# Sending the softmax reciprocals with each token's id, and a new order on VectorE behind attention, in a fused attention and mixture-of-experts kernel

## The chip, the cores and the metric

The kernel runs on one core of one Trainium2 chip. The metric is the time of one execution on the device in microseconds (us). Engines are called by the profile's letters: PE is TensorE (PEld its weight loads), DVE is VectorE, ACT is ScalarE, POOL is GpSimd, SP is the SyncE queue, which only issues DMAs here.

## What is computed

```python
def _attn_ref(q, k, v, cap):                 # 8 batches, 12 heads, 448 positions, 64 wide
    scores = scale * np.matmul(q, k.transpose(0, 1, 3, 2))
    scores = cap * np.tanh(scores / cap)
    ...
    attn = attn / (np.sum(attn, axis=-1, keepdims=True) + 1e-09)
    return np.matmul(attn, v)
def _moe_ref(x, w_gate, w1, w2):             # 3584 tokens of 768, 8 experts, F = 1024
    expert_idx = np.argmax(x @ w_gate, axis=1)
    ...
    for e in range(E):
        h = np.maximum(x[mask] @ w1[e], 0.0)
        out[mask] = gate_w[mask, None] * (h @ w2[e])
```

The output of attention, with its 12 heads side by side, is the input `x` of the experts.

## The kernel before, in words

**Attention.** The 8 batches are cut into 24 quads of four heads, a quad into 7 tiles of 64 keys. A step is two tiles. In each step PE makes two tiles of scores (`scores`, L249), ACT a tanh on each (`tanh`, L262) and one exponential on both (`expo`, L265), and PE the product with V of earlier tiles (`pv`, L315). Two score tiles fit in PSUM, so PE can be ahead of ACT by that much and no more. DVE adds the exponentials up for the softmax sums (`adds`, L270). The output is left unnormalised: the sums of a batch are made by `strips0` and `strips`, turned by `rec_t`, and `rec_v` takes their reciprocals (`rec`, one for each head and position) and scales the logits `lt` by them. What comes then is entered in `tasks` under a step and run there.

**Reciprocals before.** `rec_p` spreads the reciprocals by three products of 128x56 into PSUM, and `rec_c` copies them behind the 192 columns of `yt`, the turned output of the batch. `store` writes `yt` to the scratch table `xd` in DRAM, rows of 198 floats. So whoever gathers rows of `xd` (`load_x`) gets the six reciprocals of a row with it, and `scale_c`, `scale_k` multiply them in.

**Routing.** `log_p` makes the logits, `route_v` the expert of each token (`ob`), `route_s` and `route_g` its gate, `place_p` and `place_v` its slot, and four `place_d` scatter the token's id and gate (`tokg`) into the table `ids`, 8 bytes a row, by POOL's queue. A block of up to 448 tokens of one expert starts with `load_ids` (a gather of `ids` into `idt`), then `make_idx` on DVE (`xi`, from `idt`), then `load_x`.

**Experts.** Each block takes eight `up` (f = 0 to 7: 18 products for one slice of 128 hidden units, into `ph`) and eight `down` (18 products, into y). All operands are split in a high and a low part, so a product is (high, high), (high, low), (low, high): the third of each group needs the low part of a weight. ACT makes high parts (`high`, L797) and relu (L936), DVE low parts (`low`, L802, tiles w10l to w17l and w20l to w27l) and the hidden low parts (L937). Large blocks stream 448 columns, the two small ones at the end 256 (`up`) and 384 (`down`, L964). In `down` of a small block the hidden tile in `hb` is the stationary operand and the weight the moving one; elsewhere the weight is stationary.

**Behind attention.** The first block (j = -2, tokens of the first three batches) is run while the last batch is still being routed: its eight `up` stand between steps of the routing, in an order that is written out by hand (L1126 to L1186 before). Each engine works its own instructions in that order, so an instruction that waits holds up all behind it on its engine. `second_block` picks the expert of the second block, `tables` makes the list of all further blocks (some 45 small DVE operations), and the pads (`PADS`, L105) set how far apart tiles of weights and of operands stand in SBUF.

Of the kernel before, what the change touches and what calls it, by code (L numbers as in the profile page):

```python
# [18 lines left out]
E = 8  # L19
# [12 lines left out]
XR = XW + NP  # L32
# [15 lines left out]
C_MK = C_SM + 128  # L48
C_STRIP = C_MK + 128 * NQ
# [18 lines left out]
def consts():  # L68
# [5 lines left out]
    same = within[:, None] == within[None, :]  # L74
    c[:, C_SM : C_SM + 128] = same
    for i in range(NQ):
        c[:, C_MK + 128 * i : C_MK + 128 * i + 128] = same & (quad[:, None] == i)
# [27 lines left out]
PADS = (192, 64, 96)  # L105
# [21 lines left out]
def attention_moe(tc, qT, kT, vL, capd, wgL, w1a, w1b, w2a, w2b, cst, cmk, out):  # L127
# [21 lines left out]

    xd = dpool.tile([T * 4, XR], F32, name="xd")  # L150

    ids = dpool.tile([(E + 1) * T, 2], I32, name="ids")
# [6 lines left out]
    def load(mq, part):  # L159
# [38 lines left out]
    xg = rpool.tile([128, QB, XR], F32, name="xg")  # L198
# [18 lines left out]
    tokg = keep.tile([128, 4 * B, 2], I32, name="tokg")  # L217
    lt = att.tile([128, 16, 32], F32, name="lt")
    ob = att.tile([128, 5, E], BF16, name="ob")
# [4 lines left out]
    def constants():  # L224
        V.tensor_copy(out=kc, in_=cs[:, C_KEEP:C_N])
        V.tensor_copy(out=base, in_=kcol(C_BASE, 8))
        V.tensor_copy(out=tokg[:, :, 0], in_=cs[:, C_TOK : C_TOK + 4 * B])
        V.memset(lt, 0.0)
        V.memset(ob, 0.0)
# [94 lines left out]
    def turn(n):  # L324
        b, hp = divmod(n, NP)
        if hp == 0:

            if b in (0, 2, 4):
                yts[b] = w2r[b > 0].rearrange("p a b -> p (a b)")[:, 0 : QB * XR].rearrange("p (q x) -> p q x", x=XR)
            else:  # L330
                yts[b] = yp.tile([128, QB, XR], F32, name="yt", bufs=2)
# [44 lines left out]
    def rec_v(b):  # L376
# [4 lines left out]
        rec = fin[b, "rec"] = att.tile([128, QB, 4], F32, name="rec")  # L381
        V.reciprocal(out=rec[0:KR], in_=st[0:KR, :, 0:4])
        fill()
        l4 = lt[0:KR, 0:QB].rearrange("p q (g e) -> p q g e", e=E)
        V.tensor_tensor(out=l4, in0=l4, in1=rec[0:KR].unsqueeze(3).broadcast_to([KR, QB, 4, E]), op=ALU.mult)
        fill()

    def rec_p(b):
# [3 lines left out]
        n = QB * 4  # L392
        for i in range(NQ):
            w = cs[0:KR, C_MK + 128 * i : C_MK + 128 * i + 128]
# [977 lines left out]
```

## Time and profile before

| | us |
|---|---|
| median of 3 runs | 790.88 (790.17 to 791.96) |
| the profiled execution | 792.4 |
| its span, first to last instruction | 790.1 |
| busy: PE / DVE / ACT / POOL | 773.5 / 548.3 / 452.0 / 363.6 |

Read the stages apart: until 299 us attention, with both PE and ACT busy nearly all the time; then 50 us in which PE has work for all of the time but waits for others at a few points; from 348 us on PE is the chain that ends last, without a break until 782 us. In the timeline a number in square brackets is the engine's idle time before an instruction, with what ended it.

### The profile page before, as it was taken

The page shows a single profiled execution, that of the slowest core. Times are in us where ns is not written, and L with a number is a line of the kernel's source. Part 1 is how long each engine was busy: PE and PEld are TensorE (multiplying, and loading weights), DVE is VectorE, ACT ScalarE, POOL GpSimd, SP SyncE. Part 2 cuts the span into 40 slices and gives each one's busy share as a digit, 9 for nine tenths or more (in the row PEclk, how much of TensorE's full clock was granted, in tenths as well). Part 3 has the DMA queues.
Part 4 walks back from the last instruction along what each step waited for, and adds up shares of the span by engine and source line. Part 5 has one row for each costly group of instructions (what it writes and reads, how often), then busy time and mean ns, then how long its engine had stood idle before and what let it go on. Part 6 is the DMA issues. An engine that isn't in the chain of part 4 may idle for free.

```text
span 790.1 us, 14368 instructions
## 1 busy us (share of the span) xinstructions
PE 773.5 (98%) x5740; PEld 568.0 (72%) x5740; DVE 548.3 (69%) x943; ACT 452.0 (57%) x537; POOL 363.6 (46%) x323
## 2 busy tenths in 40 slices
PE   8999999999999999899999999999999999999996
PEld 3334343444444446789999999999999999999995
DVE  2787898999899998698548448348358357357730
ACT  7999999999999993234433333224224323334521
POOL 1000312135841302672675774774774774756601
PEclk9999999999999999999999999999999999999998
DMA  8233564558988503233264624524620225543501
GB/s 297 84 128 127 157 186 127 182 126 296 241 251 190 167 2 74 53 94 135 77 217 171 231 72 186 211 72 181 218 69 17 62 73 201 194 153 123 190 38 38
DMA packets 35018, 112.76 MB, mean 143 GB/s; under 512 B 8422, under 2 KB 14872, under 8 KB 31872
## 3 DMA queue, kind: packets, MB, share of 16 engines
q0 software_dynamic: 19152, 70.22, 26.8%
q1 hardware_dynamic: 15504, 41.32, 17.4%
q8 instruction: 47, 0.77, 0.4%
q10 hardware_dynamic: 288, 0.23, 0.1%
q14 instruction: 27, 0.22, 0.1%
HBM read 101.87 MB, written 22.85 MB: 158 GB/s over the span
## 4 chain that ended last, share of the span: by engine, by line
PE 56%; DVE 1%; issue 1%; DMA 0%; POOL 0%; ACT 0%; POOLq 0%; DVEq 0%
PE ph L926 27%; PE y L956 22%; PE y L964 4%; PE ms L956 1%; PE po L956 1%; PE z L956 1%; DMA idt<-ids,t1i 0%; DVE w21l L802 0%; DVE w22l L802 0%; POOL ids L495 0%; DVE w15l L802 0%; DVE first L680 0%; ACT w21h L797 0%; POOL out L762 0%; ACT hx L936 0%
## 5 line engine op out<-in xcount | busy, mean ns | idle before, releaser
L936 ACT ACTIVATE hb<-ph 128x448 fp32r<-128x448 f32 (+1 forms) x67 | 33.9, 507 | 257.8 <-PE ph L926 257.8
L752 POOL DMA_INDIRECT xg<-xd,xi x114 | 132.7, 1164 | 56.8 <-issue 36.5
L265 ACT ACTIVATE pt<-pt,capt 128x1792 f32<-128x1792 f32 x84 | 153.4, 1829 | 0.0
L937 DVE SCALAR_TENSOR_TENSOR hb<-ph,hb 128x448 fp32r<-128x448 f32 (+1 forms) x67 | 38.1, 569 | 163.8 <-ACT hb L936 163.8
L249 PE MATMUL sp<-qr,kr 64*64 64x448 f32 x1344 | 147.2, 547 | 3.8 <-ACT pt L262 3.7
L262 ACT ACTIVATE pt<-sp 128x896 f32<-128x896 f32 x161 | 141.0, 947 | 8.0 <-PE sp L249 7.6
L315 PE MATMUL po<-pt,vr 64*64 64x448 f32 x1344 | 144.9, 537 | 0.1
L762 POOL DMA_INDIRECT out<-ys,xi x98 | 106.3, 1085 | 30.1 <-issue 26.5
L249 PEld LDWEIGHTS sp<-qr,kr 64*64 64x64 f32 x1344 | 48.0, 133 | 84.9 <-issue 44.0
L315 PEld LDWEIGHTS po<-pt,vr 64*64 64x64 f32 x1344 | 56.1, 133 | 72.4 <-issue 61.7
L495 POOL DMA_INDIRECT ids<-tokg,slots x32 | 44.1, 1377 | 60.1 <-DVE slots L489 33.4
L270 DVE TENSOR_TENSOR acc<-acc,pt 128x1792 f32<-128x1792 f32 (+1 forms) x36 | 61.2, 1699 | 2.6 <-ACT pt L265 2.5
L463 POOL DMA_DIRECT2D xd<-w2r x12 | 8.3, 704 | 96.6 <-DVE w2r L400 96.6
L270 DVE TENSOR_TENSOR acc<-pt 128x896 f32<-128x896 f32 (+1 forms) x36 | 50.0, 1390 | 3.4 <-ACT pt L265 3.4
L901 ACT CAST xh<-xt 128x448 fp32r<-128x448 f32 (+1 forms) x54 | 27.3, 533 | 28.3 <-DVE xt L897 28.3
L322 DVE COPY ot<-po 128x448 f32<-128x448 f32 x48 | 27.6, 616 | 21.0 <-PE po L315 21.0
L463 POOL DMA_DIRECT2D xd<-yt x16 | 10.5, 664 | 62.3 <-DVE yt L400 62.3
L926 PE MATMUL ph<-xh,qr 128*128 128x448 f32 (+1 forms) x108 | 37.1, 344 | 0.0
L926 PE MATMUL ph<-xh,kr 128*128 128x448 f32 (+1 forms) x108 | 37.2, 344 | 0.0
L926 PE MATMUL ph<-xl,qr 128*128 128x448 f32 (+1 forms) x108 | 37.1, 344 | 0.0
L752 POOL DMA_INDIRECT w1r<-in_w1b,widx x7 | 9.5, 1351 | 48.8 <-DVE w17l L802 48.5
L897 DVE STREAM_TRANSPOSE xt<-xg 128x448 f32<-128x448 f32 (+1 forms) x54 | 30.3, 582 | 0.8
(395 smaller groups left out, 1811.7 us busy)
## 6 DMA issues: line engine op xcount, KB each, us to landing
vr<-in_vL SPq DMA_DIRECT2D x24, 448.0 KB, 3.6
kr<-in_kT SPq DMA_DIRECT2D x23, 448.0 KB, 5.0
qr<-in_qT SPq DMA_DIRECT2D x23, 448.0 KB, 5.9
xd<-yt POOLq DMA_DIRECT2D x16, 346.5 KB, 6.8
xd<-w2r POOLq DMA_DIRECT2D x12, 346.5 KB, 5.4
xg<-xd,xi POOLq DMA_INDIRECT x114, 3.7
out<-ys,xi POOLq DMA_INDIRECT x98, 2.3
w1r<-in_w1a SPq DMA_DIRECT2D x4, 384.0 KB, 5.7
```

The lines of the kernel that those rows point to most:

```text
L249: PE.matmul(sp[w, r, 0:S], kr[h, c, 64 * g : 64 * g + 64], qr[h, c, :], start=True, stop=True)
L262: A.activation(out=pts[t // 2][:, t % 2], in_=sps.pop(t)[:, :, 0:S], func=AF.Tanh, scale=qsc if t < KT else 1.0)
L265: A.activation(out=pts[k], in_=pts[k], func=AF.Exp, scale=capt)
L270: V.tensor_tensor(out=o, in0=a, in1=b, op=ALU.add)
L315: PE.matmul(pvs[m][c][w, 0:S], vr[r, g, j, :], pt[r, j, :], start=g == 0, stop=g == KT - 1)
L495: i = G.indirect_dma_start(out=ids, out_offset=bass.IndirectOffsetOnAxis(ap=slots[0:p, c : c + 1].bitcast(U32), axis=0), in_=tokg[0:p, c, ...
L752: G.indirect_dma_start(out=dst, out_offset=None, in_=src, in_offset=bass.IndirectOffsetOnAxis(ap=idx.bitcast(U32), axis=0), bounds_check=b ...
L762: i = G.indirect_dma_start(out=dst, out_offset=bass.IndirectOffsetOnAxis(ap=idx.bitcast(U32), axis=0), in_=src, in_offset=None, bounds_che ...
L926: PE.matmul(ph, w[:, 128 * k : 128 * k + 128], x[:, k, 0:n], start=i == 0, stop=i == 3 * KC - 1)
L936: A.activation(out=hh, in_=ph, func=AF.Relu)
L937: V.scalar_tensor_tensor(out=hl, in0=ph, scalar=0.0, in1=hh, op0=ALU.max, op1=ALU.subtract)
L956: PE.matmul(y[k][:, 0:LARGE], w[:, c], h, start=f == 0 and i == 0, stop=f == FC - 1 and i == 2)
```

## The change

Reciprocals travel with the token. An `ids` row has 14 words: id, gate, and 12 reciprocals. `rec_p` makes them in token order by twelve products of 32x16 in the place of three of 128x56, `rec_c` is one copy of 128x48 and one of 128x4 into a new `tokg`, `xd` rows have 192 floats, and `scale_c` takes two operations on 64 partitions. The fill of `ids` at the start is seven times as large, from another tile, in two DMAs. `rec` is a fixed tile that is set to zero at the start. The constants for these products are 32 columns wide in the place of 128, so the table of constants is half as wide. The first three loads of Q and K stand in another order.

Three further parts: the order behind attention (below), `tables` in pieces between the splits of w22, w23 and w24, and 32 columns (128 bytes) of offset for `hb`'s slots in small blocks; `PADS[2]` is 192 for 96.

```diff
-XR = XW + NP
+IW = 2 + H
...
-PADS = (192, 64, 96)
+PADS = (192, 64, 192)
...
-    xd = dpool.tile([T * 4, XR], F32, name="xd")
-
-    ids = dpool.tile([(E + 1) * T, 2], I32, name="ids")
+    xd = dpool.tile([T * 4, XW], F32, name="xd")
+
+    ids = dpool.tile([(E + 1) * T, IW], I32, name="ids")
...
+                nc.sync.dma_start(out=qr[:, 1], in_=qT[b, :, 1])
+                nc.scalar.dma_start(out=qr[:, 0], in_=qT[b, :, 0])
                 nc.sync.dma_start(out=kr[:, :, 0:128], in_=kT[b, :, p, 0:128])
-                nc.scalar.dma_start(out=qr[:, 0], in_=qT[b, :, 0])
-                nc.sync.dma_start(out=qr[:, 1], in_=qT[b, :, 1])
...
-        filli = w1r[0][:, 0, 0 : 2 * (E + 1) * T // 128].bitcast(I32)
+        n = IW * (E + 1) * T // 256
+        filli = w1r[1].rearrange("p a b -> p (a b)")[:, 0:n].bitcast(I32)
         V.memset(filli, 1 << 20)
         G.memset(xg, 0.0)
-        nc.sync.dma_start(out=ids.rearrange("(p a) o -> p (a o)", p=128), in_=filli)
+        iv = ids.rearrange("(h p a) o -> h p (a o)", h=2, p=128)
+        for half in range(2):
+            nc.sync.dma_start(out=iv[half], in_=filli)
...
-        n = QB * 4
         for i in range(NQ):
-            w = cs[0:KR, C_MK + 128 * i : C_MK + 128 * i + 128]
-            PE.matmul(pm[:, n * i : n * i + n], w, fin[b, "rec"][0:KR], start=True, stop=True)
+            for a in range(4):
+                PE.matmul(
+                    pm[32 * a : 32 * a + 32, 16 * i : 16 * i + 16],
+                    cs[0:KR, C_MK + 32 * i : C_MK + 32 * i + 32],
+                    rec[0:KR, a::4, :],
+                    start=True,
+                    stop=True,
+                )
+
+    tokgs = {}
     def rec_c(b):
-        for j in range(2):
-            r = slice(64 * j, 64 * j + 64)
-            V.tensor_copy(
-                out=yts[b][r, :, XW : XW + NP].rearrange("p q (i c) -> p i q c", c=2),
-                in_=fin[b, "rp"][r, 0 : NQ * QB * 4].rearrange("p (i q c j) -> p j i q c", q=QB, c=2, j=2)[:, j],
-            )
-            fill()
+        tg = tokgs[b] = keep.tile([128, 4, IW], I32, name="tokg", bufs=2)
+        V.tensor_copy(out=tg[:, :, 0], in_=cs[:, C_TOK + 4 * b : C_TOK + 4 * b + 4])
+        V.tensor_copy(
+            out=tg[:, :, 2:IW].bitcast(F32).rearrange("p t (i m) -> p t i m", m=4),
+            in_=fin[b, "rp"][:, 0 : 16 * NQ].rearrange("p (i t m) -> p t i m", t=4, m=4),
+        )
...
-            in_=tokg[0:p, c, :],
+            in_=tokgs[b][0:p, q, :],
...
-        V.tensor_tensor(
-            out=sc[:, 0:c],
-            in0=xg[:, 0:c, XW : XW + NP],
-            in1=t[:, 0:c, 1].bitcast(F32).unsqueeze(2).broadcast_to([128, c, NP]),
-            op=ALU.mult,
-        )
+        for i in range(2):
+            tf = t[64 * i : 64 * i + 64, 0:c].bitcast(F32)
+            V.tensor_tensor(
+                out=sc[64 * i : 64 * i + 64, 0:c],
+                in0=tf[:, :, 2 + i : IW : 2],
+                in1=tf[:, :, 1].unsqueeze(2).broadcast_to([64, c, NP]),
+                op=ALU.mult,
+            )
...
-            b, s = m["hb"], 2 * n * (f % (3 if n == LARGE else 5))
+            b, s = m["hb"], 2 * n * (f % 3) if n == LARGE else 2 * n * (f % 5) + 32
...
     strips(b)
     rec_t(b)
+    rec_v(b)
     for k in range(2):
         do(STEPS + 4 + k, "v")
     assert not tasks
+    up(-2, 2)
+    split_w1(4)
     second_block()
     load_ids(-1)
     load_w(-1, 0, [0])
-    up(-2, 2)
-    rec_v(b)
-    split_w1(4)
     up(-2, 3)
-    make_idx(-1)
-    load_x(-1)
     rec_p(b)
     log_p(b)
     split_w1(5)
+    rec_c(b)
     route_v(b)
     route_s(b)
     up(-2, 4)
     split_w1(6)
-    rec_c(b)
+    make_idx(-1)
+    load_x(-1)
     turn(b * NP + 4)
     turn(b * NP + 5)
     store(b, nc.sync)
...
+    tb = tables()
+
+    def some(n):
+        while n and next(tb, 0):
+            n -= 1
+
     up(-2, 6)
     split_w2(1)
-    for _ in tables():
-        pass
+    some(14)
+    split_w2(2)
     up(-2, 7)
-    split_w2(2)
+    some(14)
     split_w2(3)
+    some(-1)
     load_w(-1, 0, [1])
```

On DVE, right behind attention's last adds, before: the two transposes of `rec_t`, then `route_g` of the batch before, two turns, and `second_block`.

```order
L370 STREAM_TRANSPOSE lt<-ms 128x448
L373 STREAM_TRANSPOSE st<-ms 128x448
L454 TENSOR_REDUCE gt<-ex 128x4
L456 TENSOR_SCALAR gt<-gt 128x4
L458 RECIPROCAL tokg<-gt 128x4
L333 STREAM_TRANSPOSE yt<-ot 128x14x32 x2
L544 SCALAR_TENSOR_TENSOR cnt_2939<-fbo,k_1704,cnt_2939 128x8
```

The same place on DVE in the changed kernel.

```order
L373 STREAM_TRANSPOSE lt<-ms 128x448
L376 STREAM_TRANSPOSE st<-ms 128x448
L382 COPY st<-st 64x14x2
L383 COPY st<-lt 32x14x4
L384 RECIPROCAL rec<-st 96x56
L387 TENSOR_TENSOR lt<-lt,rec 96x448
L462 TENSOR_REDUCE gt<-ex 128x4
L464 TENSOR_SCALAR gt<-gt 128x4
L466 RECIPROCAL tokg<-gt 128x4
L336 STREAM_TRANSPOSE yt<-ot 128x14x32 x2
L947 SCALAR_TENSOR_TENSOR hb<-ph,hb 128x448
L810 TENSOR_TENSOR w14l<-w1r_122,w14h 128x768
```

The four operations of `rec_v` now stand ahead of `route_g`, and a hidden low part and w14l ahead of `second_block`.

Further on DVE, where `xi` (from the gathered ids `idt`) is made, before.

```order
L826 MEMSET idt 128x28
L937 SCALAR_TENSOR_TENSOR hb<-ph,hb 128x448
L379 COPY st<-st 64x14x2
L380 COPY st<-lt 32x14x4
L382 RECIPROCAL rec<-st 96x56
L385 TENSOR_TENSOR lt<-lt,rec 96x448
L802 TENSOR_TENSOR w14l<-w1r_122,w14h 128x768
L937 SCALAR_TENSOR_TENSOR hb<-ph,hb 128x448
L840 TENSOR_SCALAR xi<-idt,kc 128x14
L802 TENSOR_TENSOR w15l<-w1r_122,w15h 128x768
L437 TENSOR_REDUCE mx<-ms 128x4
```

The same place on DVE in the changed kernel, from w15l on.

```order
L810 TENSOR_TENSOR w15l<-w1r_122,w15h 128x768
L408 CAST tokg<-cs 128x4
L409 COPY tokg<-ms 128x4x12
L445 TENSOR_REDUCE mx<-ms 128x4
L447 TENSOR_TENSOR df<-ms,mx 128x32
L433 SCALAR_TENSOR_TENSOR tkc<-df,kc 128x32
L435 TENSOR_REDUCE tkm<-tkc 128x4
L438 TENSOR_TENSOR tko<-kc,tkm 128x32
L451 TENSOR_TENSOR ob<-tko,cs 128x32
L947 SCALAR_TENSOR_TENSOR hx<-ph,hx 128x448
L810 TENSOR_TENSOR w16l<-w1r_122,w16h 128x768
L848 TENSOR_SCALAR xi<-idt,kc 128x14
```

`xi` now stands behind w15l, the copies of `rec_c`, the six operations of `route_v`, a hidden low part and w16l.

Then DVE in the middle of `tables`, in the changed kernel; before, w22l stood behind all of `tables` and a hidden low part.

```order
L643 TENSOR_TENSOR le<-cb,kc 128x64
L651 TENSOR_REDUCE ej<-le 128x19
L655 TENSOR_TENSOR le<-le,nbe 128x88
L810 TENSOR_TENSOR w22l<-w2r_123,w22h 128x768
L947 SCALAR_TENSOR_TENSOR hx<-ph,hx 128x448
L662 TENSOR_REDUCE pr<-le 128x11
L664 TENSOR_TENSOR pr<-kc,pr 128x11
L668 SCALAR_TENSOR_TENSOR le<-kc,ej 128x64
```

w22l is made after 14 operations of `tables`, and w23l after 14 more.

## Rows read from the trace of the kernel before

**Rows 1.** Windows: us, busy us of PE, PEld, DVE, ACT, POOL; PEclk, DMA share, GB/s
```profile
310.00:350.00 40.00, 36.44 (x216) 31.90 (x209) 32.23 (x111) 14.34 (x22) 24.80 (x23) 0.96 0.32 78
376.00:714.00 338.00, 338.00 (x1692) 316.90 (x1691) 193.76 (x301) 116.97 (x184) 219.74 (x192) 1.00 0.40 142
```

**Rows 2.** Waits of TensorE, whole span: line <- releaser: us in total, times, longest
```profile
PE ph L926 <- DVE w15l L802: 2.0, 1, 2.0
PE ms L395 <- DVE rec L382: 0.8, 1, 0.8
PE z L956 <- DVE w22l L802: 0.7, 1, 0.7
```

**Rows 3.** ScalarE's timeline in attention: start, us, line, operation [idle before <-releaser]
```profile
102.65 1.83 ACT L265 ACTIVATE pt<-pt,capt 128x1792 f32<-128x1792 f32 x1
...
105.93 1.84 ACT L265 ACTIVATE pt<-pt,capt 128x1792 f32<-128x1792 f32 x1
107.98 1.73 ACT L262 ACTIVATE pt<-sp 128x896 f32<-128x896 f32 x2 [0.21 <-PE sp L249]
109.59 1.79 ACT L265 ACTIVATE pt<-pt,capt 128x1792 f32<-128x1792 f32 x1
...
178.27 1.84 ACT L265 ACTIVATE pt<-pt,capt 128x1792 f32<-128x1792 f32 x1
...
182.07 1.79 ACT L265 ACTIVATE pt<-pt,capt 128x1792 f32<-128x1792 f32 x1
```

**Rows 4.** TensorE's timeline in that step, a batch's reciprocals and logits
```profile
105.74 0.88 PE L395 MATMUL ms<-rec,cs 96*128 96x56 f32 x6
106.54 0.46 PE L411 MATMUL ms<-lt,cs 96*32 96x32 f32 x32
```

**Rows 5.** TensorE's timeline behind attention
```profile
319.54 0.84 PE L395 MATMUL ms<-rec,cs 96*128 96x56 f32 x6 [0.83 <-DVE rec L382]
...
326.97 0.47 PE L926 MATMUL ph<-xh,w15l 128*128 128x448 f32 x1 [1.98 <-DVE w15l L802]
...
328.11 0.57 PE L926 MATMUL ph<-xh,w15h 128*128 128x448 f32 x1
328.49 0.57 PE L926 MATMUL ph<-xl,w15h 128*128 128x448 f32 x1
```

**Rows 6.** VectorE's timeline behind attention
```profile
318.46 0.18 DVE L379 COPY st<-st 64x28 f32<-64x28 f32 x1
...
319.97 0.95 DVE L802 TENSOR_TENSOR w14l<-w1r,w14h 128x768 fp32r<-128x768 f32 x1
...
325.82 0.23 DVE L840 TENSOR_SCALAR xi<-idt,kc 128x14 int32<-128x14 int32 x1 [4.37 <-DMA idt<-ids,t1i]
325.97 0.95 DVE L802 TENSOR_TENSOR w15l<-w1r,w15h 128x768 fp32r<-128x768 f32 x1
...
330.29 1.17 DVE L333 STREAM_TRANSPOSE yt<-ot 128x448 f32<-128x448 f32 x2
332.64 0.62 DVE L937 SCALAR_TENSOR_TENSOR hx<-ph,hx 128x448 fp32r<-128x448 f32 x1 [1.18 <-ACT hx L936]
...
334.49 0.95 DVE L802 TENSOR_TENSOR w17l<-w1r,w17h 128x768 fp32r<-128x768 f32 x1
...
373.50 0.62 DVE L937 SCALAR_TENSOR_TENSOR hb<-ph,hb 128x448 fp32r<-128x448 f32 x1 [0.87 <-ACT hb L936]
```

**Rows 7.** ScalarE's timeline at 341 us
```profile
341.25 0.83 ACT L797 CAST w23h<-w2r 128x768 fp32r<-128x768 f32 x1 [0.48 <-DMA xg<-xd,xi]
```

**Rows 8.** The chain that ended last, in order of time, merged: start, us, what
```profile
412.48 3.60 PE y L956 x18
...
718.97 2.10 PE y L964 x12
721.06 2.12 PE ph L926 x18
```

**Rows 9.** VectorE's timeline at the start
```profile
13.48 0.48 DVE L232 MEMSET w1r<- 128x504 int32 x1
```

More of the change, by code (lines that the diff above doesn't have):

```diff
@@ L73, in consts @@
     quad, within = p // 32, p % 32
-    same = within[:, None] == within[None, :]
-    c[:, C_SM : C_SM + 128] = same
+    same = within[:, None] == np.arange(32)
+    c[:, C_SM : C_SM + 32] = same
     for i in range(NQ):
-        c[:, C_MK + 128 * i : C_MK + 128 * i + 128] = same & (quad[:, None] == i)
+        c[:, C_MK + 32 * i : C_MK + 32 * i + 32] = same & (quad[:, None] == i)
     c[:64, C_STRIP + 31] = 1.0
@@ L197, in attention_moe @@
     w2r = [rpool.tile([128, FC // 2, DM], F32, name=f"w2r{i}") for i in range(2)]
-    xg = rpool.tile([128, QB, XR], F32, name="xg")
+    xg = rpool.tile([128, QB, XW], F32, name="xg")
     warm = w1r[0][:, 2, 0:128].bitcast(BF16)
@@ L216, in attention_moe @@
     slots = keep.tile([128, 4 * B], I32, name="slots")
-    tokg = keep.tile([128, 4 * B, 2], I32, name="tokg")
     lt = att.tile([128, 16, 32], F32, name="lt")
+    rec = att.tile([128, 16, 4], F32, name="rec")
     ob = att.tile([128, 5, E], BF16, name="ob")
@@ L226, in constants @@
         V.tensor_copy(out=base, in_=kcol(C_BASE, 8))
-        V.tensor_copy(out=tokg[:, :, 0], in_=cs[:, C_TOK : C_TOK + 4 * B])
         V.memset(lt, 0.0)
+        V.memset(rec, 0.0)
         V.memset(ob, 0.0)
-        filli = w1r[0][:, 0, 0 : 2 * (E + 1) * T // 128].bitcast(I32)
+        n = IW * (E + 1) * T // 256
+        filli = w1r[1].rearrange("p a b -> p (a b)")[:, 0:n].bitcast(I32)
         V.memset(filli, 1 << 20)
         G.memset(xg, 0.0)
-        nc.sync.dma_start(out=ids.rearrange("(p a) o -> p (a o)", p=128), in_=filli)
+        iv = ids.rearrange("(h p a) o -> h p (a o)", h=2, p=128)
+        for half in range(2):
+            nc.sync.dma_start(out=iv[half], in_=filli)
     pts = {}
@@ L328, in turn @@
             if b in (0, 2, 4):
-                yts[b] = w2r[b > 0].rearrange("p a b -> p (a b)")[:, 0 : QB * XR].rearrange("p (q x) -> p q x", x=XR)
+                yts[b] = w2r[b > 0].rearrange("p a b -> p (a b)")[:, 0 : QB * XW].rearrange("p (q x) -> p q x", x=XW)
             else:
-                yts[b] = yp.tile([128, QB, XR], F32, name="yt", bufs=2)
+                yts[b] = yp.tile([128, QB, XW], F32, name="yt", bufs=2)
         c = 32 * hp
@@ L380, in rec_v @@
         V.tensor_copy(out=st[64:96, :, 0:4], in_=lt[96:128, 0:QB, 0:4])
-        rec = fin[b, "rec"] = att.tile([128, QB, 4], F32, name="rec")
-        V.reciprocal(out=rec[0:KR], in_=st[0:KR, :, 0:4])
+        V.reciprocal(out=rec[0:KR, 0:QB], in_=st[0:KR, :, 0:4])
         fill()
         l4 = lt[0:KR, 0:QB].rearrange("p q (g e) -> p q g e", e=E)
-        V.tensor_tensor(out=l4, in0=l4, in1=rec[0:KR].unsqueeze(3).broadcast_to([KR, QB, 4, E]), op=ALU.mult)
+        V.tensor_tensor(out=l4, in0=l4, in1=rec[0:KR, 0:QB].unsqueeze(3).broadcast_to([KR, QB, 4, E]), op=ALU.mult)
         fill()
@@ L457, in route_g @@
         fill()
-        V.reciprocal(out=tokg[:, 4 * b : 4 * b + 4, 1].bitcast(F32), in_=gt)
+        V.reciprocal(out=tokgs[b][:, :, 1].bitcast(F32), in_=gt)
     def store(b, e):
@@ L823, in load_ids @@
         c = groups(j)
-        t = keep.tile([128, QB, 2], I32, name="idt", bufs=2)
+        t = keep.tile([128, QB, IW], I32, name="idt", bufs=2)
         if j < 0:
```

6 lines of the change are left out of this document (3 added, 3 removed).

## The prediction

> **What bounds the kernel now.** First the windows [rows 1]: from 376 to 714 us PE is busy for all of the 338 us, while DVE has 194 and ACT 117. Whatever the change does there on other engines, smaller gathers of `xd` and larger ones of `ids` included, lies beside PE work and is worth nothing as long as PE's own pace stays. Between 310 and 350 us PE is busy for 36.4 of 40 us at a mean clock of 0.96. The list of PE's waits says which operations it waits for there [rows 2]: the low part of w15, `rec`, the low part of w22, 3.5 us together. [...] In attention the reader is to compare starts of the exponential [rows 3]: 3.28 us apart in an ordinary step, 3.66 and 3.80 in steps in which PE also runs `rec_p` and `log_p`; ACT sets the pace, and where PE gets extra work it sits idle for scores.
>
> **Part 1: reciprocals by token, in attention.** Before, a batch's `rec_p` holds PE from 105.74 to 106.54, 0.80 us [rows 4]. The new form is 12 products, in two passes each as the other fp32 ones (6 for 3, 32 for 16), so 24 passes of 16 columns. The nearest row is the logits' 32 passes, also with 96x32 weights: 0.46 us, 14 ns a pass, so 24 x 14 = 0.35 us. A batch saves 0.45 us of PE. What does ACT get of it? The excess of such a step over 3.27 is 0.29 to 0.53 us in the first five batches (0.39 and 0.53 in the two shown [rows 3]; the others 0.29, 0.29, 0.29), sum 1.8. All five are about as large as the saving, so I take 1.8, and 0.1 for each of five later steps in which PE's lead, rebuilt from a smaller debt, covers more of `strips0`: **2.3 us**. The ends: 0.8 if each small product costs twice as much and the lead is short again right behind it; 3.2 if all seven batches save the full 0.45. [...]
>
> On DVE `rec_c` gets shorter (two copies of 64x84 become one of 128x48 and one of 128x4) by some 0.15 us a batch, which counts once, where `strips` of the last batch waits for DVE. `scale_c` in two operations costs 0.2 us in a block, beside PE work of 58 us a block. The fill grows from 504 to 1764 elements a partition: 0.48 us becomes 1.7 [rows 9], ahead of a scaling of Q whose scores come three steps later; the two DMAs stand on SP ahead of loads needed at 40 us. Both are covered; if not, the start loses up to 1 us. The order of the first three loads changes nothing I can price: the first score tile needs all three. I allow 0.3 us either way.
>
> **Part 2: the order behind attention.** `rec` no longer stands behind `second_block`: the wait of 0.83 goes, and `rec_p` saves its 0.45 here too. Then w15l. Before, `xi` stands ahead of it, and DVE sits idle 4.37 us for the gathered ids [rows 6]; w15l ends at 326.92. With `xi` out of the way it ends 4.37 + 0.15 + 0.15 sooner, at 322.2. PE, ahead by the first gains, wants it at 323.3, so the 1.98 us go, and with them the slow products: from 327.74 to 331 us ten of them lost 0.17 each, 1.75 us. Gain at the end of `up` 5: 0.83 + 0.45 + 1.98 + 1.75 + 0.15 (DVE) = 5.2, and 0.1 for a restart.
>
> What is late next is w17l. `xi` still waits for the ids, and these come later: `rec_v`, 1.51 us long (318.46 to 319.97 [rows 6]), now stands ahead of the gate of batch 6, hence of its four scatters and of the gather behind them on POOL. `xi` can start at 325.8 + 1.5 - 0.15 + 0.3 (a row of ids is seven times as long) = 327.5. DVE gets there at 325.5, after `rec_c`, `route_v`, a hidden low part and w16l (0.35 + 1.3 + 0.7 + 0.9 from 322.2). Queued behind that wait are the turns, the store of the last batch, `place_v` and w17l. From the turns to the end of w17l DVE has 335.44 - 330.29 - 1.18 idle = 4.0 us of work [rows 6]: w17l ends at 331.6. PE wants it at 330.7: **a new wait of 0.9 us**, too short, as the 0.83 before, to cost clock. Gain now 4.4.
>
> w22l: before it stood behind all of `tables` and cost 0.74 us and restarts, 1.1 with all. Now it stands behind 14 operations. But by the tiles' addresses in the two built programs, w22h now shares memory with `yt` of the last batch (before, w23h was the first to), so it must wait until that store has landed: in the trace 9.8 us after the turns (331.46 to 341.25 [rows 6, 7]), so at about 338.5 here. DVE loses 2.2 us of idle time there, w22l ends at 340.2, PE wants it at 342.4: covered with 2.2 us to spare. +1.1, gain 5.5.
>
> Then DVE. It has no gap in the trace from `tables` to the first hidden part of the second block, where it is 0.87 us early (the row at 373.50 [rows 6]). It is to start this stretch 4.2 us sooner, less 2.2 of the new wait, less 0.2 of `scale_c`: that part is ready at 371.4. PE would want it at 371.0: 0.45 us lost. **Part 2 in all: 5.0 us.** The ends: 2.5, if ids or store land 2 us later than taken (each us late then costs one); 6.2, if neither new wait comes.
>
> **Part 3: the offset of `hb` in small blocks.** From the addresses, the stationary tile begins 192 bytes past a multiple of 256 from the moving one in every `up` and `down`, except in `down` of small blocks: 64 there, 192 after. The chain gives 0.1178 us a product at 256 columns, 0.200 at 448, so 0.1726 at 384 on the line between; measured is 0.175 [rows 8]. If the whole difference is the distance, 2 blocks x 96 products x 2.4 ns = **0.5 us**; ends 0 and 1.5. [...] No row here decides it: width and distance change together.
>
> **Sum.** 2.3 + 5.0 + 0.5 = 7.8 us. The profiled execution took 792.4 us, 2.3 more than its span; this gives 784.6 and a span of 782.3. It was 1.5 us above the median of the runs, so from 790.88: **783.1 us**.
>
> **The rivals.** *A, as summed*, 0.55: 780.5 to 785. *B, attention gains little* (the small products are not cheaper, or PE's lead is spent in the next step anyway): 0.8 for 2.3, 784.6; 0.15. For it: it would take only 20 ns more a pass; against it: the logits' row. *C, the order only moves the waits*: the ids land 2 us later than taken, or the store does, and DVE's wait for `xi` or w22h passes on to PE with its clock: 0.9 becomes 2.9 and 1.75 comes back, part 2 is 1.2, in all 786.9; 0.17. For it: all three of DVE's late tiles hang on one gather. *D, slower, by layout*: almost all weight and operand tiles move, by 352 or 1632 bytes. The pace of 0.200 us holds for some 1,900 products of 448 columns behind attention. It decides from 4.1 ns a product (2%): at 5 ns the price is 9.5 us and the time 792.6; 0.06. Against it: the distances modulo 256 are the same before and after for all of them, and it would be the first effect of that size in this trace. *E, no change*: C and B together with half of D, about 790; 0.07.
>
> **How the numbers follow.** The time is A's. Two in ten may lie outside, so the range reaches from A's lower end with the upper ends of parts 1 and 2, 780.0, to C's 787.6. A measurement of this kernel tells about 0.2%, 1.6 us, from no change. Faster by more: A, B and C, 0.87; within: E, 0.07; slower: D, 0.06.
>
> **What would show it.** Right: steps with `rec_p` at 3.27 to 3.4 us; no PE wait for w15l or `rec`, no stretch at the lower clock behind attention; a short wait for w17l; DVE idle before `xi` for about 2 us and before w22l; `down` of small blocks at 0.1726 us. Wrong: steps still at 3.56; a PE wait of over 2 us behind attention; `up` and `down` of large blocks off 0.200.

## The result and the profile after

The changed kernel takes 784.07 us in the median of six runs (781.37 to 786.49), the kernel before 791.42 (790.17 to 793.61): a ratio of 0.9904, 95% interval 0.9877 to 0.9931. The forecast was 783.1 with a range of 780.0 to 787.6. The profiled execution took 782.08 us with a span of 780.1; the sum had said 784.6 and 782.3. So this one execution gained 10.3 us where 7.8 were predicted, and the medians 7.35. The two differences from 7.8 have different causes, which are taken up below.

| place in the trace (us) | before | after | shift |
|---|---|---|---|
| start of the first tanh on scores | 7.17 | 6.50 | -0.67 |
| start of the last exponential | 297.23 | 293.93 | -3.30 |
| first product of `down` 0 of the first block | 339.30 | 330.54 | -8.76 |
| first product of `up` of the second block | 369.12 | 359.34 | -9.78 |
| end of the span | 790.09 | 780.13 | -9.96 |

The windows that answer to [rows 1] (same columns): PE has no idle time any more between 310 and 350 us, and its clock is 1.00 for 0.96. In the kernel before the granted clock was 0.50 from 328 to 331 us, behind the wait of 1.98 us for w15l, and the products there were 0.37 to 0.38 us apart [rows 5].

```profile
310.00:350.00 40.00, 40.00 (x257) 36.99 (x256) 35.66 (x118) 13.73 (x22) 28.17 (x25) 1.00 0.30 74
376.00:714.00 338.00, 338.00 (x1717) 317.51 (x1716) 198.82 (x318) 116.37 (x185) 223.78 (x195) 1.00 0.40 143
```

The list of PE's waits, to be held against [rows 2]: w15l, `rec` and w22l are gone. What is left stands at the start (scores, warm-up) and in attention, where the last two lines are new, at 291 and 254 us: there PE is now 0.6 us ahead of ACT and of DVE.

```profile
PE sp L252 <- ACT pt L265: 3.8, 6, 1.6
PE sp L205 <- DVE qsc L209: 1.1, 1, 1.1
PE sp L252 <- issue: 0.7, 1, 0.7
PE ph L936 <- ACT pt L265: 0.6, 1, 0.6
PE po L318 <- DVE ot L325: 0.6, 1, 0.6
```

PE's timeline in the step of [rows 4] and, third row, behind attention, as in [rows 5]:

```profile
104.67 0.38 PE L396 MATMUL ms<-rec,cs 96*32 96x16 f32 x24
104.88 0.47 PE L419 MATMUL ms<-lt,cs 96*32 96x32 f32 x32
...
314.97 0.38 PE L396 MATMUL ms<-rec,cs 96*32 96x16 f32 x24
315.18 0.67 PE L419 MATMUL ms<-lt,cs 96*32 96x32 f32 x32
```

The 24 small passes hold PE for 0.21 us (104.67 to 104.88) where the six wide ones held it for 0.80, and no wait stands in front of 314.97. ACT's timeline in the steps of [rows 3]: from 104.86 to 108.13 and from 176.22 to 179.49 the exponentials are 3.27 us apart, where 3.66 and 3.80 stood.

```profile
101.58 1.82 ACT L268 ACTIVATE pt<-pt,capt 128x1792 f32<-128x1792 f32 x1
...
104.86 1.84 ACT L268 ACTIVATE pt<-pt,capt 128x1792 f32<-128x1792 f32 x1
...
108.13 1.86 ACT L268 ACTIVATE pt<-pt,capt 128x1792 f32<-128x1792 f32 x1
...
176.22 1.84 ACT L268 ACTIVATE pt<-pt,capt 128x1792 f32<-128x1792 f32 x1
...
179.49 1.86 ACT L268 ACTIVATE pt<-pt,capt 128x1792 f32<-128x1792 f32 x1
```

DVE's timeline behind attention, against [rows 6]:

```profile
317.94 0.95 DVE L810 TENSOR_TENSOR w15l<-w1r,w15h 128x768 fp32r<-128x768 f32 x1
...
322.30 0.23 DVE L848 TENSOR_SCALAR xi<-idt,kc 128x14 int32<-128x14 int32 x1 [0.29 <-DMA idt<-ids,t1i]
...
325.71 0.95 DVE L810 TENSOR_TENSOR w17l<-w1r,w17h 128x768 fp32r<-128x768 f32 x1
...
334.23 0.96 DVE L810 TENSOR_TENSOR w22l<-w2r,w22h 128x768 fp32r<-128x768 f32 x1 [1.63 <-ACT w22h L805]
```

The wait for w22h is there as forecast (1.63 us, covered). The wait of `xi` is 0.29 us, where the prediction had 2 and a wait of PE for w17l behind it. That is the first surprise.

### The profile page after: what moved, and what is told of

Read it like the earlier page. It is cut to its first block, busy times and chain, and to the rows that moved or that the text cites. A ratio compares the mean times of both kernels' runs of the same rounds, so it can differ in the third digit from the quotient of the medians.

```text
span 780.1 us, 14674 instructions
## 1 busy us (share of the span) xinstructions
PE 765.6 (98%) x5884; PEld 562.7 (72%) x5884; DVE 549.0 (70%) x952; ACT 451.3 (58%) x537; POOL 367.4 (47%) x323
## 4 chain that ended last, share of the span: by engine, by line
PE 64%; DVE 3%; ACT 2%; issue 0%; POOL 0%; POOLq 0%; DVEq 0%; ACTq 0%
PE ph L936 30%; PE y L966 22%; PE y L974 4%; PE po L318 2%; PE ms L966 1%; PE po L966 1%; PE z L966 1%; DVE acc L273 1%; PE sp L252 1%; ACT pt L268 1%; ACT pt L265 1%; PE ms L355 0%; DVE p L273 0%; DVE ot L325 0%; PE ms L347 0%
## 5 line engine op out<-in xcount | busy, mean ns | idle before, releaser
L760 POOL DMA_INDIRECT xg<-xd,xi x114 | 135.0, 1184 | 55.7 <-issue 38.1
L770 POOL DMA_INDIRECT out<-ys,xi x98 | 108.3, 1105 | 29.9 <-issue 27.7
L915 DVE TENSOR_TENSOR xl<-xt,xh 128x448 fp32r<-128x448 f32 (+1 forms) x54 | 28.7, 556 | 0.0
```

What stands on the lines that cost most here:

```text
L760: G.indirect_dma_start(out=dst, out_offset=None, in_=src, in_offset=bass.IndirectOffsetOnAxis(ap=idx.bitcast(U32), axis=0), bounds_check=b ...
L770: i = G.indirect_dma_start(out=dst, out_offset=bass.IndirectOffsetOnAxis(ap=idx.bitcast(U32), axis=0), in_=src, in_offset=None, bounds_che ...
```

## The experiments

Medians in us; the ratio is to the kernel before, run beside each on the same chip.

| kernel | median (range), runs | ratio, 95% interval |
|---|---|---|
| after_again | 782.35 (781.95 to 784.92), 5 | 0.9902, 0.9885 to 0.9919 |
| after_old_order | 786.23 (785.51 to 787.54), 5 | 0.9947, 0.9933 to 0.9961 |
| after_no_offset | 784.20 (782.12 to 784.58), 5 | 0.9912, 0.9896 to 0.9928 |
| after_old_loads | 784.08 (783.45 to 784.49), 4 | 0.9916, 0.9901 to 0.9931 |
| before_wide_ids | 792.89 (790.20 to 793.86), 10 | 1.0017, 1.0001 to 1.0033 |
| before_new_order | 787.66 (787.31 to 788.06), 8 | 0.9959, 0.9943 to 0.9975 |
| after_q_first | 782.66 (781.51 to 784.09), 6 | 0.9897, 0.9876 to 0.9919 |
| after_double_rec | 784.64 (783.71 to 786.05), 4 | 0.9925, 0.9898 to 0.9952 |
| before_wide_again | 788.27 (787.95 to 790.35), 8 | 0.9971, 0.9959 to 0.9984 |
| after_dist_64 | 784.42 (784.26 to 785.86), 4 | 0.9930, 0.9913 to 0.9947 |
| after_dist_0 | 788.87 (787.58 to 789.55), 8 | 0.9975, 0.9963 to 0.9987 |
| after_dist_128 | 787.11 (786.16 to 787.47), 4 | 0.9956, 0.9940 to 0.9973 |

Medians move by up to 2 us with things that are not the edit, at the start of the execution among others, as the first three experiments show. So a stage is read from the profiles between marks of its own: *attention* from the first exponential to the last, *behind attention* from the last exponential to the first `up` of the second block.

| us | attention | behind attention |
|---|---|---|
| before | 286.15 | 71.89 |
| before_wide_ids | 287.96 | 70.21 |
| before_wide_again | 286.17 | 68.30 |
| before_new_order | 286.14 | 67.13 |
| after_old_order | 284.56 | 68.04 |
| after | 283.52 | 65.41 |
| after_again | 283.51 | 65.41 |
| after_q_first | 283.50 | 65.40 |
| after_double_rec | 284.25 | 65.91 |

### Where the spread comes from: the start

**after_again.** 

> The changed kernel once more, unaltered. Its six executions so far lie between 781.37 and 786.49 us with mean granted clocks from 0.998 down to 0.992, and the one that was profiled (782.08, 0.998) has hardly a product at the lower clock. Theory: the spread is PE's clock in one stretch; the profile of this run, if it falls in an execution of 784 us or more, shows 2 to 4 us of products at 0.37 us in the place of 0.20 us, either at the start (where PE waits for the first scores) or behind attention. Rival: the time is lost without the clock, in waits for DMAs; then the clock stays at 0.998 and a wait of 2 us or more stands in the list of PE's waits. Median expected 783 to 785 either way.

Measured: 782.35 us. The profile fell in an execution with a clock of 0.999, so this run alone decided nothing. Two of the other four executions show 0.994 and 0.995, and they are the two slowest (784.92, 783.34).

**after_old_loads.**

```diff
-                nc.sync.dma_start(out=qr[:, 1], in_=qT[b, :, 1])
+                nc.sync.dma_start(out=kr[:, :, 0:128], in_=kT[b, :, p, 0:128])
                 nc.scalar.dma_start(out=qr[:, 0], in_=qT[b, :, 0])
-                nc.sync.dma_start(out=kr[:, :, 0:128], in_=kT[b, :, p, 0:128])
+                nc.sync.dma_start(out=qr[:, 1], in_=qT[b, :, 1])
```

> The changed kernel with the first three loads of Q and K in the order of before. Theory (the load order gave the 0.67 us by which the first tanh is earlier, 6.50 against 7.17 us): first tanh at 7.1 to 7.2 us, and the time 0.6 to 0.7 us longer. Rival (the prediction's: the first score tile needs all three loads, so the order is worth nothing, and the 0.67 us came from the smaller table of constants or from chance): first tanh at 6.5 us and the same time.

Measured: first tanh at 7.10 us and 784.08 us, which looks like the theory. But the order of the loads is not what decides: with the new order the first tanh stands at 6.50 us in one profile, 7.17 in after_again, 6.11 in after_no_offset. In `after` and after_no_offset the first 16 score products take 1.74 us, in after_again and after_old_loads 2.35. In after_again the first two groups of four take 0.77 and 0.65 us and the third 0.37, which looks like a lower clock; in after_old_loads 0.52 us lie behind the first product alone, where a load can be missing. The column of the granted clock reads 1.00 here in `after`, after_again and after_no_offset, so neither cause is shown. What the order is worth stays open; the spread is larger than its effect.

The slow stretch itself is in the profiles of after_no_offset, after_old_order and after_old_loads. PE's timeline of after_no_offset, and the windows behind it:

```profile
12.75 0.98 PE L252 MATMUL sp<-qr,kr 64*64 64x448 f32 x8 [1.59 <-ACT pt L265]
15.38 1.77 PE L252 MATMUL sp<-qr,kr 64*64 64x448 f32 x8 [1.65 <-ACT pt L268]
16.90 2.36 PE L318 MATMUL po<-pt,vr 64*64 64x448 f32 x16
```

```profile
14.00:16.00 2.00, 0.62 (x4) 0.34 (x8) 1.98 (x3) 2.00 (x2) 0.00 (x0) 0.71 0.52 205
16.00:18.00 2.00, 2.00 (x16) 0.82 (x12) 1.93 (x2) 0.96 (x2) 0.00 (x0) 0.50 1.02 409
18.00:20.00 2.00, 2.00 (x24) 0.79 (x20) 0.17 (x1) 1.80 (x2) 0.00 (x0) 0.94 1.06 332
```

Eight products, then 1.65 us of nothing, then a granted clock of 0.50 from 16 to 18 us, and ACT busy there for only 0.96 of the two us. In the profiled execution of the changed kernel the same gap is 0.69 us and the clock stays at 1.00. The list calls the releaser "issue" or `pt`; DVE's timeline of after_no_offset names it. The eight products of the second quad need its scaled Q:

```profile
11.89 0.23 DVE L225 COPY kc<-cs 128x123 f32<-128x123 f32 x1 [6.33 <-DMA cs<-in_cst]
...
13.27 1.53 DVE L233 MEMSET w1r<- 128x1764 int32 x1 [0.32 <-issue]
14.72 0.56 DVE L260 TENSOR_SCALAR qr<-qr,qsc 128x896 f32<-128x896 f32 x1
```

The scaling ends at 15.28, the products start at 15.38. Ahead of it stands the fill of `ids`, 1.53 us for 0.48 before [rows 9]. How long PE waits depends on when the table of constants lands (its first copy starts at 11.3 to 12.1 us in these profiles) relative to the first scores: that copy starts 0.86 to 1.84 us ahead of the first eight products, and this lead and PE's wait add up to 2.51 us in all five profiles. The mean clock of the first 20 us is 1.00 with a wait of 0.69 us in `after` and 0.67 in after_again, and 0.91 with 0.91 (after_old_loads), 1.09 (after_old_order) and 1.65 (after_no_offset).

**after_q_first.**

```diff
-    at(0, "v", constants)
-    for q in range(1, QUADS):
+    at(0, "v", scale_q, 1)
+    at(0, "v", constants)
+    for q in range(2, QUADS):
```

> The changed kernel with one thing moved: the scaling of Q for the second quad stands ahead of the constants on VectorE, so it no longer waits for the table of constants and for the fill of 1.53 us. Theory (the fill, three times as long as before, makes PE wait 0.7 to 1.7 us for that scaling at 14 to 15 us, and PE falls to its lower clock there in some executions, which is the spread of 781.4 to 786.5): no wait of PE between its 40th and 41st score product, granted clock 0.998 or more, median 781 to 782, no execution above 783. Rival (the slow stretch comes from the loads of the third quad or from chance, and the scaling only happens to stand there): spread and median as those of the changed kernel, 782 to 784.5.

Measured: PE's timeline has the 16 products in one row and the windows a clock of 1.00.

```profile
13.52 1.88 PE L252 MATMUL sp<-qr,kr 64*64 64x448 f32 x16 [1.59 <-ACT pt L265]
15.21 1.68 PE L318 MATMUL po<-pt,vr 64*64 64x448 f32 x16
```

```profile
14.00:16.00 2.00, 2.00 (x28) 0.70 (x24) 0.81 (x1) 2.00 (x3) 0.00 (x0) 1.00 0.48 189
16.00:18.00 2.00, 1.91 (x24) 0.54 (x20) 1.93 (x1) 2.00 (x4) 0.00 (x0) 1.00 1.00 393
```

The granted clock is 0.997 to 0.999 in all six executions; in the changed kernel five of eleven have 0.992 to 0.995, and these are five of the six slowest. The kernels below that are built on this one bear it out: with the scaling first, none of 22 executions has less than 0.996, while 11 of the 29 of the changed kernel and its variants without it have 0.995 or less. So the theory of the gap stands. The forecast of the time does not: the median is 782.66, and three executions with a clock of 0.997 or 0.998 took 783.20, 783.57 and 784.09, where none above 783 was expected. The mean over the changed kernel's eleven executions is 783.5, over these six 782.7, which are not told apart. What these three lose, no profile shows; the first products wait for the load of K by a varying amount (1.06 us in this profile, 1.15 in after_dist_128, none listed in `after`), which is a candidate and no more. This is the version I would keep, but it isn't shown to be faster.

### What the order is worth, and what the width of an `ids` row is

**after_old_order**: the changed kernel with the order of before behind attention.

```diff
     rec_t(b)
-    rec_v(b)
...
-    up(-2, 2)
-    split_w1(4)
     second_block()
     load_ids(-1)
     load_w(-1, 0, [0])
+    up(-2, 2)
+    rec_v(b)
+    split_w1(4)
     up(-2, 3)
+    make_idx(-1)
+    load_x(-1)
     rec_p(b)
...
-    rec_c(b)
     route_v(b)
...
     split_w1(6)
-    make_idx(-1)
-    load_x(-1)
+    rec_c(b)
     turn(b * NP + 4)
...
     up(-2, 6)
     split_w2(1)
-    some(14)
-    split_w2(2)
+    for _ in tables():
+        pass
     up(-2, 7)
-    some(14)
+    split_w2(2)
     split_w2(3)
-    some(-1)
```

> The changed kernel with the order behind attention as it was before (second block's choice, xi, reciprocals, tables at their old places); reciprocals by token, pads and offset stay. Theory (the order is worth what the profile shows, 6.5 us up to the second block): 790 to 791 us, the waits for w15l (about 2 us) and rec (0.8) are back, and PE at its lower clock behind the first of them. The prediction's own figure for it, 5.0, gives 789.1. Rival (the order only moves waits, and the gain behind attention comes from part 1): 784 to 786 us, with other waits in the place of those for w15l and rec.

Measured: 786.23 us, and 68.04 us behind attention, 2.63 more than with the new order. This is less than the theory and the prediction's figure, and more than the rival's, because the stall at w15l did not come back. PE's waits in this kernel:

```profile
PE ms L396 <- DVE rec L384: 1.2, 1, 1.2
...
PE z L966 <- DVE w22l L810: 0.8, 1, 0.8
...
PE ms L419 <- DVE lt L387: 0.2, 1, 0.2
```

Something else in the change takes the stall at w15l away. The trace says where to look: `xi` waits only 2.15 us in this kernel, with the old order, against 4.37 [rows 6]. POOL's timeline, first of the kernel before and then of after_old_order: the last of the four scatters into `ids` and the gather behind them.

```profile
318.25 0.92 POOL L495 DMA_INDIRECT ids<-tokg,slots  x1 [0.30 <-issue]
323.24 1.05 POOL L752 DMA_INDIRECT idt<-ids,t1i  x1 [4.07 <-issue]
```

```profile
315.27 0.91 POOL L503 DMA_INDIRECT ids<-tokg,slots  x1 [0.30 <-issue]
318.17 1.06 POOL L760 DMA_INDIRECT idt<-ids,t1i  x1 [1.99 <-DVE lt L387]
```

The same four scatters are followed by a gap of 4.07 us where a row has 8 bytes and of 1.99 where it has 56.

**before_new_order**: the kernel before with the changed order alone (the reverse of the diff above, on the old reciprocals and 8-byte rows).

> The kernel before with the changed kernel's order behind attention alone (8-byte rows of ids, old reciprocals, old pads and offset). Theory (8-byte rows land 2 us later): the prediction's step comes true here, xi waits about 2 us and PE waits 0.5 to 1 us for w17l; the stall for w15l is gone, and the time is 785.5 to 786.5 us. Rival (the rows' width does not matter, the new order itself brings the gather forward): POOL waits 2.0 us between scatter and gather, xi waits under 0.5 us, no wait for w17l, 784.5 to 785.5 us. Second rival (the order only moves waits): 788 us or more.

Measured: 787.66 us, 1.2 us over the theory, but 67.13 behind attention, 4.76 less than before, and step by step close to what the prediction had said. The gap on POOL is 3.99 us, `xi` waits 2.35 and w17l is late:

```profile
327.90 0.23 DVE L840 TENSOR_SCALAR xi<-idt,kc 128x14 int32<-128x14 int32 x1 [2.35 <-DMA idt<-ids,t1i]
```

```profile
331.93 0.47 PE L926 MATMUL ph<-xh,w17l 128*128 128x448 f32 x1 [0.89 <-DVE w17l L802]
```

The wait of 0.89 for w17l, forecast at 0.9, exists in this kernel, and the clock from 330 to 350 us is 1.00. What hid it in the changed kernel is the width of the rows, which the prediction had entered with the wrong sign, as 0.3 us more.

**before_wide_ids**: the kernel before with twelve words more in each row of `ids`.

```diff
-    ids = dpool.tile([(E + 1) * T, 2], I32, name="ids")
+    ids = dpool.tile([(E + 1) * T, IW], I32, name="ids")
...
-            in_=tokg[0:p, c, :],
+            in_=tokw[0:p, 2 * c : 2 * c + IW],
...
-        t = keep.tile([128, QB, 2], I32, name="idt", bufs=2)
+        t = keep.tile([128, QB, IW], I32, name="idt", bufs=2)
```

> The kernel before with 56-byte rows in the table of ids in the place of 8-byte rows (twelve words more that nobody reads; fill, scatter and gather as wide as in the changed kernel), its order and its reciprocals unaltered. Theory (the width of a row decides how soon the four scatters have landed and the gather behind them may start): POOL's idle time between the last scatter and the gather of idt falls from 4.07 us to 2.0, xi waits 2.2 us instead of 4.37, the wait of 2.0 for w15l goes and with it the products at the lower clock, together 3.5 to 4 us: 786.5 to 787. Rival (something else of the change, such as the narrower rows of xd or the shifted steps of the batch ahead, sets that time): 4.07 stays, the wait for w15l stays, 790 to 791 us. In both the longer fill delays the second scaling of Q.

Measured: the gap on POOL falls to 2.01 us, `xi` waits 2.14, the wait for w15l is gone; yet the time is 792.89, slower than before. The profile shows three other things. The longer fill opens the gap at the start (clock 0.57 from 16 to 20 us). PE waits 1.17 us for `rec` and runs at 0.50 between 324 and 326. And `down` in large blocks takes 202.0 ns a product for 199.95: by the tiles' addresses in the built program, the wider `idt` had moved w21 to w27 by 128 bytes modulo 256 against `hb`. That cost about 2.2 us over the blocks and is taken up below.

**before_wide_again**: the same with the pad of that pool at 224 for 96 bytes, which restores the distance, and with the scaling of Q first.

> The kernel before with 56-byte rows of ids once more, without the two things that came in with them by accident: the tiles of w21 to w27 stand again as far from hb as before (192 past a multiple of 256 bytes; in the first trial it was 64, and down took 202.0 ns a product for 199.95), and the second scaling of Q stands ahead of the fill. Theory (row width alone): POOL waits 2.0 us for 4.07 between scatters and gather, xi waits 2.1 to 2.2 us, no wait for w15l, down back at 200.0 ns a product, and the time 787 to 788.7 us, by whether the wait for rec (1.2 us) costs clock. Rival (the 2 us come back as other waits ahead of the second block): 789.5 us or more at 200.0 ns a product.

Measured: 788.27 us, `down` at 199.95 ns, a gap of 2.00 on POOL, `xi` 2.25 us, no wait for w15l, and this time a clock of 1.00 from 310 to 350 us, with the 1.2 us for `rec` in it. Behind attention 68.30 us, 3.59 less than before. POOL's last scatter and the gather behind it:

```profile
317.78 0.91 POOL L501 DMA_INDIRECT ids<-tokg,slots  x1 [0.30 <-issue]
320.70 1.06 POOL L758 DMA_INDIRECT idt<-ids,t1i  x1 [2.00 <-DVE lt L391]
```

So behind attention the order alone is worth 4.76 us, the width alone 3.59, and together with the rest 6.48: either of them removes the stall at w15l and the slow products behind it (1.98, and 1.75 by the prediction's estimate), and it can be removed only once. With the wide rows in place, the order brings 2.63. By the medians these two changes are worth less than by the stages: 2.74 us for the order alone (790.40 to 787.66) and 2.39 for the width alone (790.66 to 788.27); the one profiled execution of the kernel before, at 792.4, lies about 2 us above these medians.

The traces also say something of where the gap comes from. With 56-byte rows the landing of one of these four scatters is on record in after_old_order and in before_wide_ids, 2.0 and 2.1 us behind its issue, 1.1 us behind the end of its instruction. With 8-byte rows there is a single landing in the trace of before, of a scatter of the last batch (347.2 us), 4.3 us behind its issue, 2.84 behind the end; with 56-byte rows scatters of that batch landed 2.5 us behind their issue in the median of `after`. So the narrow rows seem to land later, but one landing is little to go by.

### What the cheaper reciprocals are worth

**after_double_rec.**

```diff
-        for i in range(NQ):
+        for i in [0, 1, 2] * 2:
             for a in range(4):
                 PE.matmul(
```

> The changed kernel with the twelve products of the reciprocals made twice in every batch: 24 more passes, 0.2 us of PE more a batch. Theory (in steps with these products PE is what the exponential waits for, so its time counts in full): steps with reciprocals are 0.2 us longer, five or six of them, and one behind attention, so 1.0 to 1.4 us over the changed kernel. Rival (PE has slack again after the change, the saved time was partly not needed): steps stay at 3.27 us, and the time is within 0.3 us of the changed kernel's.

Measured: attention is 0.74 us longer than in after_again, 0.50 are lost behind it, 1.24 in all, inside the theory's 1.0 to 1.4 (the median is 2 us higher, but the start lies within that). Not as the theory said, though: of the five steps with reciprocals two stay at 3.27 us and three grow by 0.08 to 0.14, and three of the `strips0` steps that follow grow by 0.11 to 0.19, the other two by 0.02 at most. About half of 7 x 0.21 us is paid in attention, and part of it a step or two late.

### The offset of `hb`, and the distance between two tiles

**after_no_offset.**

```diff
-            b, s = m["hb"], 2 * n * (f % 3) if n == LARGE else 2 * n * (f % 5) + 32
+            b, s = m["hb"], 2 * n * (f % 3) if n == LARGE else 2 * n * (f % 5)
```

> The changed kernel without the 32 columns of offset for hb's slots in small blocks, nothing else changed. Theory (distance of the two operands modulo 256 bytes counts): down of the small blocks goes back from 0.1735 to 0.175 us a product, the stage of the small blocks is 0.3 to 0.5 us longer, 784.4 to 784.6 in the median. Rival (the two operands do not disturb each other): down stays at 0.1735 us a product and the time is the same as that of the changed kernel within 0.1 us.

Measured: the small blocks, from the last product of the large ones to the last product of all, take 67.49 us, as in the kernel before; with the offset they take 67.16 in after, after_again, after_old_loads, after_old_order and after_q_first. A small `down` product has 176.0 ns without and 173.6 with it. The chain in order of time, a group of 12 such products: after_no_offset first, then `after`.

```profile
710.39 2.10 PE y L974 x12
```

```profile
709.18 2.08 PE y L974 x12
```

The part is worth 0.33 us and does what it says. The medians could not have told (784.20 against 782.35 is the start).

The accident in before_wide_ids asked for a direct trial. The three kernels differ from after_q_first in one number, the pad ahead of w21 to w27.

```diff
-PADS = (192, 64, 192)
+PADS = (192, 64, 320)
```

**after_dist_64.** 

> The kernel with the scaling of Q first (after_q_first), the tiles of w21 to w27 128 bytes further on and nothing else: the stationary tile of down then begins 64 bytes past a multiple of 256 from the moving one, in large blocks and in small ones, where it was 192. Theory (this distance sets the pace): large down 202.0 ns a product in the mean (202.3 where the moved tiles are used) for 200.0, small down 176 for 173.6, the time 2.3 to 2.6 us above after_q_first, about 785.2. Rival (the distance is not the cause, 202.0 in the first trial with wide rows came from something else there): 200.0 and 173.6 ns, time as after_q_first.

**after_dist_0** (256). 

> As after_dist_64, with the tiles 64 bytes further on: distance 0 in large blocks, 128 in small ones. Theory 1 (of the four distances only 64 is slow): 200.0 and 173.6 ns a product, time as after_q_first. Theory 2 (192 is the one good place): 201 to 203 ns and 175 to 177, time 1 to 3 us above after_q_first. Theory 3 (a better place exists): under 199.5 ns, over 0.5 us faster.

**after_dist_128** (128). 

> As after_dist_64, with the tiles 64 bytes back: distance 128 in large blocks, 0 in small ones. The same three theories: 200.0 and 173.6 ns with the time of after_q_first (only 64 is slow); 201 to 203 and 175 to 177 with 1 to 3 us more (only 192 is good); under 199.5 ns and over 0.5 us faster (a better place exists).

The chain in order of time, one group of 18 `down` products each: after_q_first (192), then distance 64, 128 and 0.

```profile
446.24 3.60 PE y L966 x18
```

```profile
446.84 3.64 PE y L966 x18
```

```profile
440.42 3.68 PE y L966 x18
```

```profile
440.44 3.72 PE y L966 x18
```

From the starts of the products, by weight tile (w21 to w27; w20 was not moved and stays at 200.0 in all of them):

| stationary begins so many bytes past a multiple of 256 from the moving tile | ns a product, 448 columns | median over after_q_first, us |
|---|---|---|
| 192 | 200.0 | 0 |
| 64 | 202.0 | 1.8 |
| 128 | 204.2 | 4.5 |
| 0 | 206.7 | 6.2 |

The second theory holds for large blocks, at a higher price than its 201 to 203 ns: 192 is the one good place of the four. It is the distance and not the place of the weight tile alone: by the built programs the moved weight tiles begin 64 bytes past a multiple of 256 in the kernel before and 160 in the changed one, both at distance 192 and both at 200.0 ns; at distance 64 they begin at 192 in before_wide_ids (202.3 ns) and at 32 in after_dist_64 (202.0). There are 882 such products (7 large blocks x 144 x 7/8), and 882 x 6.7 ns = 5.9 us agrees with the 6.2 measured. For small blocks it fails: distance 64 gave 176.0 ns in the kernel before and in after_no_offset, and 173.2 in after_dist_64, where both tiles lie 128 bytes further on than in after_no_offset. So in those the distance alone does not decide, and what does is open.

## Why the prediction was right, and where it was not

**Part 1, attention: 2.3 forecast, 2.63 measured** (286.15 to 283.52). The five steps with reciprocals are at 3.27 us, a gain of 1.8 as summed; the five `strips0` steps gave 0.5 together, as summed, but unevenly (0.11 in three, 0.19 in one, nothing in one); one step near the end gave 0.36 more. The estimate of 0.35 us for the new products was too high: 0.21, 9 ns a pass. That PE time in these steps is worth ACT time is shown by the doubled products, at about half its size.

**Fill covered: wrong.** The prediction said that the fill of 1.7 us stands ahead of a scaling "whose scores come three steps later", and that otherwise up to 1 us is lost. PE waits for that scaling by 0.7 to 1.7 us, and with the waits of 0.91 us and more the mean clock of the first 20 us is 0.91; attention is 1.0 to 1.6 us longer there (284.56 in after_old_order, 284.58 in after_old_loads, 285.13 in after_no_offset, against 283.5). The step that failed is the time: PE comes to those scores, the eighth tile, at 13.7 to 14.8 us, while the fill, behind the table of constants, and then the scaling end only at 14.7 to 15.5.

**Part 2, the order: 5.0 forecast, 6.48 measured.** The terms that it removes came as summed: `rec`, w15l, the slow products, and about 1.0 for w22l (28.80 us from `down` 0 to the second block, for 29.82). The covered wait for w22h came too: 1.63 us on DVE for 2.2. The new loss of 0.9 for w17l did not come, because the gather of ids followed its scatters 2 us sooner than in the trace of before: the term "+ 0.3 (a row of ids is seven times as long)" had the wrong sign and should have been -2. With 8-byte rows the 0.9 was there (0.89). The further 0.45 at the second block's first hidden part hung on the same late DVE and did not come. Rival C priced a gather 2 us later than taken; it was the other end of the same unknown that came. The remark that w23h was the first tile to share memory with `yt` before is not right: by the built program w22l shared it too, and in before_new_order it is w22l that waits for the store, 1.97 us.

**Part 3, the offset: 0.5 forecast, 0.33 measured.** Inside a group a product gained the 2.4 ns, 0.42 us together; 0.09 came back where groups meet and in `up`. The straight line between two widths was a fair estimate. That the place of the two tiles to each other has a price, which no row had decided, was measured: 0.33 us here, and 200.0 against 206.7 ns a product with nothing moved but the weight tiles.

**Rival D, slower by layout** did not come, since `PADS[2]` had moved with the tiles, but before_wide_ids ran into such a price by accident: 202.0 ns a product for 199.95, about 2.2 us.

**The sum.** Against the profiled execution: 0.67 at the start, 2.63 + 6.48 for 2.3 + 5.0, 0.33 for 0.5, together 10.1; the large blocks took 0.15 more, the span shrank by 9.96 and the time by 10.3 us. The 0.67 can't be put down to the change: the first tanh stands anywhere from 6.1 to 7.4 us in the profiles.

Against the median, 7.35 for 7.8, neither side is like its profile. Six of the eleven executions of the changed kernel lose 1 to 4 us that the profiled one did not. The three profiles with a slow start show 1.0 to 1.6 us of that; where the rest goes is open. And the profiled execution of the kernel before (792.4, granted clock 0.995) lies 1 to 2 us above that kernel's medians (791.42, 790.42, 790.40, 790.66). Of its 45 executions in the experiments 32 have a clock of 0.996 or more, so most may lack the 1.75 us of slow products behind w15l; no profile of one is there to tell. The prediction took the 1.5 us above the median off its base, and still counted the 1.75 in the gain. So it is partly luck that the median came within 1 us of the forecast: a gain that was 2.5 too small in the profiled pair, a start that was not covered, and a base that does not hold all of the gain nearly cancelled.

Two sums of the prediction don't come out. Its lower end of 780.0 takes the upper end of part 3 too; those of parts 1 and 2 alone give 781.0. And rival E's C, B and half of D make about 793 and not 790.

## What to carry to other kernels

A transfer that is made larger need not hold up its reader for longer: here the gather followed scatters of 56-byte rows after 2.0 us and of 8-byte rows after 4.0. Read from the trace when the next reader starts, and try another width. An instruction that is lengthened at the start of a program has to be held against the first wait of every engine there, in more than one execution: here a fill of 1.53 us for 0.48 left a gap of 0.67 to 1.65 us on PE, with a mean clock of 0.91 over the first 20 us where the gap was 0.91 us or more, and this makes a part of the spread. And before the cause of a slowdown is sought in what was changed, compare the pace of products that were not: in before_wide_ids tiles that had moved by 128 bytes cost about 2.2 us, more than the 1.68 us that the edit gained there behind attention (71.89 to 70.21).

## What the runs showed of the hardware

- Behind attention the gather that reads the table followed the last of four scatters of 8-byte rows after 4.07 us (before) and 3.99 (before_new_order), of 56-byte rows after 1.99 to 2.01 (after, after_old_order, after_q_first, after_double_rec, before_wide_ids, before_wide_again). What takes the 2 us was not tried, nor any width between.
- The pace of the 448-column products of `down` went with where the stationary tile begins from the moving one, modulo 256 bytes: 200.0, 202.0, 204.2 and 206.7 ns a product at distances 192, 64, 128 and 0 (after_q_first, after_dist_64, after_dist_128, after_dist_0).
- Waits of like length were followed by different clocks. Behind 1.17 us for `rec` in before_wide_ids the clock was 0.81 from 322 to 324 us and 0.50 from 324 to 326; with a wait for `rec` of 1.16 us in after_old_order and of 1.2 in before_wide_again it was 1.00 from 310 to 350 us. Behind 0.83 us in before it was 1.00 (319 to 322 us), with 0.89 in before_new_order 1.00 (330 to 350 us); at the start, with 0.91 us in after_old_loads, it was 0.91 over the first 20 us.
- The warm-up products into `sp` do not keep one pace in all executions: the last eight of the twenty, from 3.60 us on, took 1.92 us in `after`, where they are 214 ns apart to the end, 1.52 in after_no_offset and 1.17 in after_q_first. The column of the granted clock reads 1.00 there in all three, so the difference is read from the pace alone.
